# Opening gates of a row tile: sums by width chunk, first loads on two queues, a shorter warm-up

## The chip, the cores and the metric

The kernel runs on one core of one Trainium2 chip. The metric is the device time of one execution in microseconds (us); medians over several executions are given.

## The reference

```python
x = A_x                                   # 2048 rows x 640, bf16
xn = layernorm(x)                         # no scale, no bias
s = attention(xn, k_cache, v_cache, wq, wo)     # 32 heads of 192, last 512 keys
g = silu( (sigmoid(xn @ w_gate) * (xn @ w_up)) @ w_down )   # inner width 1536
return x + s * g
```

Only the gated part, and of it only the first block of 512 rows, is touched here. The width of 640 is five chunks of 128. The inner width of 1536 is twelve pieces of 128; the first four are called f = 0 to 3.

## The kernel before

TensorE is the bound. The kernel does the gated part first, because it needs only x and three weights, and hides the loads for attention behind it. At the very start nothing has been loaded yet, so the first 512 rows are opened row tile by row tile (128 rows each): `tile_gates` computes the first four pieces of the gate and up products of one row tile as soon as its rows are normalized and transposed. When all four tiles are in, the normal 512-row matmuls take over (`gated`).

The loads at the start, all on SyncE's queue:

```python
        nc.vector.memset(warm[:], 0.0)
        load_x(0, 1)
        load_x(1, 1)
        for f0, f1 in ((0, 4), (4, 8), (8, NF)):
            load_f(nc.sync, wg_sb, wg_r, f0, f1)
            load_f(nc.sync, wu_sb, wu_r, f0, f1)
            if f0 == 0:
                load_x(2, 1)
                load_x(3, 1)
```

The warm-up matmuls, the transpose of one row tile by TensorE with its copy out of PSUM (the memory that holds the sums of matmuls, `bank` in the code), and the opening of one row tile:

```python
        def dummy(n):
            for _ in range(n):
                nc.tensor.matmul(bank[2][:, 1, 0:256], lhsT=warm[:, 0:P], rhs=warm[:, 0:256],
                                 start=True, stop=True)
        # ... row statistics (stats_half, stats_end) and normalization (normal): VectorE ...
        def turn_pe(t, c0, c1, bk, eng):
            pT = bk[:, 0:NCD * H2].bitcast(BF16).rearrange("p (c n) -> p c n", c=NCD)
            for c in range(c0, c1):
                nc.tensor.transpose(pT[:, c, :], ln[t][:, c * P:(c + 1) * P], ident[:])
            dst = xnT[:, 0, c0:c1, t * P:(t + 1) * P]
            if eng is nc.vector:
                nc.vector.tensor_copy(dst, pT[:, c0:c1, :])
            else:
                nc.scalar.activation(dst, pT[:, c0:c1, :], AF.Copy)
        # ... cut ...
        def tile_gates(t, amid):

            if 0 not in hT:
                hT[0] = hpool.tile([P, NF, TB], BF16, name="hT")
            k = t % 3
            r = slice(t * P, (t + 1) * P)
            for half, w in ((0, wg_sb), (1, wu_sb)):
                for f in range(FT):
                    if (half, f) == (1, 2) and amid is not None:
                        turn_pe(amid, 0, NCD, bank[3][:, amid % 2, :], nc.scalar)
                    for c in range(NCD):
                        nc.tensor.matmul(bank[k][:, half, f * P:(f + 1) * P],
                                         lhsT=w[:, c, f * P:(f + 1) * P], rhs=xnT[:, 0, c, r],
                                         start=(c == 0), stop=(c == NCD - 1))
            sig = bwork.tile([P, TB], BF16, name="sig")
            nc.scalar.activation(sig[:], bank[k][:, 0, :], AF.Sigmoid)
            nc.vector.tensor_tensor(hT[0][:, 0:FT, r],
                                    bank[k][:, 1, :].rearrange("p (f n) -> p f n", f=FT),
                                    sig[:].rearrange("p (f n) -> p f n", f=FT), ALU.mult)
```

The program order of the opening, which is also the order on each engine:

```python
        dummy(20)
        full_stats(0)
        normal(0, ((0, 3 * P), (3 * P, D)))
        turn_pe(0, 0, 3, bank[3][:, 0, :], nc.vector)
        turn_pe(0, 3, NCD, bank[2][:, 0, :], nc.scalar)
        dummy(2)
        stats_half(1, 1)
        stats_end(1)
        normal(1)
        full_stats(2)
        tile_gates(0, 1)
        normal(2)
        full_stats(3)
        tile_gates(1, 2)
        normal(3)
        tile_gates(2, 3)
        tile_gates(3, None)
        k = 1
        for f in range(FT, NF):
            gated(0, f, k, norm_piece(1, f - FT))
            k = (k + 1) % 4
        # ... the rest of the kernel: unchanged ...
```

The softmax here doesn't subtract the row's maximum and nothing guards it: scores larger than these inputs give would overflow.

Of the kernel before, what the change touches and what calls it, by code (L numbers as in the profile page):

```python
# [8 lines left out]
AF = mybir.ActivationFunctionType  # L9
ALU = mybir.AluOpType  # L10
BF16 = mybir.dt.bfloat16
# [4 lines left out]
def kernel(  # L16
# [13 lines left out]
    nc = tc.nc  # L30
    P = 128
    H2 = 64
# [16 lines left out]
    NCD = D // P  # L49
    NF = F // P  # L50
# [19 lines left out]
    bank = [psum.tile([P, 2, 512], F32, name=f"bank{i}") for i in range(4)]  # L70
# [4 lines left out]
    ident = const.tile([P, P], BF16, name="ident")  # L75
# [3 lines left out]
    warm = const.tile([P, 512], BF16, name="warm")  # L79

    xnT = pers.tile([P, NB, NCD, TB], BF16, name="xnT")
# [5 lines left out]
    wg_r = B_w_gate.rearrange("(c p) f -> p c f", p=P)  # L87
    wu_r = B_w_up.rearrange("(c p) f -> p c f", p=P)
# [45 lines left out]
    with ExitStack() as bctx:  # L134
# [5 lines left out]
        wg_sb = wB.tile([P, NCD, F], BF16, name="wg_sb")  # L140
        wu_sb = wB.tile([P, NCD, F], BF16, name="wu_sb")
# [4 lines left out]
        def load_x(t, n):  # L146

            x = xpool.tile([P, n, D], BF16, name=f"x_sb{n}", bufs=4 if n == 1 else 2)
            nc.sync.dma_start(x[:], xf[t * P:(t + n) * P, :].rearrange("(q p) d -> p q d", p=P))  # L149
            for i in range(n):  # L150
                xt[t + i] = x[:, i, :]

        def load_f(eng, w, r, f0, f1):
            eng.dma_start(w[:, :, f0 * P:f1 * P], r[:, :, f0 * P:f1 * P])  # L154

        nc.vector.memset(warm[:], 0.0)
        load_x(0, 1)
        load_x(1, 1)
        for f0, f1 in ((0, 4), (4, 8), (8, NF)):
            load_f(nc.sync, wg_sb, wg_r, f0, f1)  # L160
            load_f(nc.sync, wu_sb, wu_r, f0, f1)
            if f0 == 0:
                load_x(2, 1)
                load_x(3, 1)
        load_x(TQ, TQ)
        nc.sync.dma_start(wd_sb[:], wd_r)
        load_x(2 * TQ, TQ)
# [6 lines left out]

        def dummy(n):
            for _ in range(n):
                nc.tensor.matmul(bank[2][:, 1, 0:256], lhsT=warm[:, 0:P], rhs=warm[:, 0:256],
                                 start=True, stop=True)

        ln = {}  # L180

        def stats_half(t, i):
            if i == 0:
                ln[t] = bwork.tile([P, 2, nc.vector.BN_STATS_DIM], F32, name="st")
            nc.vector.bn_stats(ln[t][:, i, :], xt[t][:, i * (D // 2):(i + 1) * (D // 2)])

        def stats_end(t):
            mv = bwork.tile([P, nc.vector.BN_AGGR_DIM], F32, name="mv")
            rstd = bwork.tile([P, 1], F32, name="rstd")
            nc.vector.bn_aggr(mv[:], ln[t][:])  # L190
            if t == 0:
                nc.scalar.activation(rstd[:], mv[:, 1:2], AF.Sqrt, bias=eps_t[:], scale=1.0)
                nc.scalar.activation(junk[:], eps_t[:], AF.Sigmoid)
                stats_half(1, 0)
                nc.vector.reciprocal(rstd[:], rstd[:])
            else:
                nc.vector.tensor_scalar(rstd[:], mv[:, 1:2], eps, None, op0=ALU.add)
                nc.gpsimd.tensor_tensor(rstd[:], rstd[:], mhalf[:], ALU.pow)
            ln[t] = mv, rstd

        def normal(t, parts=((0, D),)):
            mv, rstd = ln[t]
            xn = xpool.tile([P, D], BF16, name="xn")
            for d0, d1 in parts:
                nc.vector.tensor_scalar(xn[:, d0:d1], xt[t][:, d0:d1], mv[:, 0:1], rstd[:, 0:1],
                                        op0=ALU.subtract, op1=ALU.mult)
            ln[t] = xn

        def turn_pe(t, c0, c1, bk, eng):
            pT = bk[:, 0:NCD * H2].bitcast(BF16).rearrange("p (c n) -> p c n", c=NCD)  # L210
            for c in range(c0, c1):
                nc.tensor.transpose(pT[:, c, :], ln[t][:, c * P:(c + 1) * P], ident[:])  # L212
            dst = xnT[:, 0, c0:c1, t * P:(t + 1) * P]
            if eng is nc.vector:
                nc.vector.tensor_copy(dst, pT[:, c0:c1, :])
            else:
                nc.scalar.activation(dst, pT[:, c0:c1, :], AF.Copy)  # L217

        def turn_dma(t):
            q = t % TQ  # L220
# [2 lines left out]
        hT = {}  # L223
# [41 lines left out]
        FT = 4  # L265

        def tile_gates(t, amid):

            if 0 not in hT:
                hT[0] = hpool.tile([P, NF, TB], BF16, name="hT")  # L270
            k = t % 3
            r = slice(t * P, (t + 1) * P)
            for half, w in ((0, wg_sb), (1, wu_sb)):
                for f in range(FT):
                    if (half, f) == (1, 2) and amid is not None:
                        turn_pe(amid, 0, NCD, bank[3][:, amid % 2, :], nc.scalar)
                    for c in range(NCD):
                        nc.tensor.matmul(bank[k][:, half, f * P:(f + 1) * P],  # L278
                                         lhsT=w[:, c, f * P:(f + 1) * P], rhs=xnT[:, 0, c, r],
                                         start=(c == 0), stop=(c == NCD - 1))  # L280
            sig = bwork.tile([P, TB], BF16, name="sig")
            nc.scalar.activation(sig[:], bank[k][:, 0, :], AF.Sigmoid)
            nc.vector.tensor_tensor(hT[0][:, 0:FT, r],
                                    bank[k][:, 1, :].rearrange("p (f n) -> p f n", f=FT),
                                    sig[:].rearrange("p (f n) -> p f n", f=FT), ALU.mult)

        def full_stats(t):
            stats_half(t, 0)
            stats_half(t, 1)
            stats_end(t)  # L290

        dummy(20)
        full_stats(0)
        normal(0, ((0, 3 * P), (3 * P, D)))
        turn_pe(0, 0, 3, bank[3][:, 0, :], nc.vector)
        turn_pe(0, 3, NCD, bank[2][:, 0, :], nc.scalar)
        dummy(2)
        stats_half(1, 1)
        stats_end(1)
        normal(1)  # L300
        full_stats(2)
        tile_gates(0, 1)
        normal(2)
        full_stats(3)
        tile_gates(1, 2)
        normal(3)
        tile_gates(2, 3)
        tile_gates(3, None)
        k = 1
        for f in range(FT, NF):  # L310
            gated(0, f, k, norm_piece(1, f - FT))
            k = (k + 1) % 4
        for b in range(1, NB):
            for f in range(2):
                gated(b, f, k)
                k = (k + 1) % 4
            for q in range(TQ):
                down(b - 1, q, k)
                k = (k + 1) % 4
            if b == 1:  # L320
                load_x(3 * TQ, TQ)
            for f in range(2, NF):
                gated(b, f, k, norm_piece(b + 1, f - 4) if b + 1 < NB and f >= 4 else None)
                k = (k + 1) % 4
# [4 lines left out]
        for q in range(TQ):  # L329
            down(NB - 1, q, k)  # L330
            k = (k + 1) % 4
# [12 lines left out]
        for m in range(DJ):  # L344
# [3 lines left out]
            k = (k + 1) % 4  # L348
# [168 lines left out]
```

## Time and profile before

| | before |
|---|---|
| time, median of 4 runs of the first comparison | 931.91 us |
| span of the profiled run | 930.2 us |
| first gate matmul of tile 0 starts | 6.94 us |
| first 512-row gate matmul starts | 18.53 us |

By the profile's page TensorE is busy 922.3 of 930.2 us (99%). The view by windows of the kernel before shows where the rest is (columns: start and end in us, length, then busy time and instruction count of TensorE's matmuls, its weight loads, VectorE, ScalarE and GpSimd, then the granted TensorE clock, the DMA engines' share and GB/s).

```profile
0.00:19.00 19.00, 16.17 (x205) 13.91 (x206) 9.29 (x27) 7.49 (x13) 2.53 (x12) 1.00 0.95 303
19.00:920.00 901.00, 901.00 (x7796) 529.67 (x7795) 451.44 (x702) 296.98 (x318) 123.92 (x142) 1.00 0.36 77
```

Between 19 and 920 us TensorE is busy all the time. So whatever the change does, it can only move the moment at which this full stretch begins.

Next the timeline of TensorE's matmuls in the opening. The columns are: start, length, engine and line, operation, output<-inputs, shape, how many are merged into the row, and in brackets how long the engine was idle before it and what ended the idle time. Line 177 is the warm-up, 212 the transposes, 278 `tile_gates`, 231 the 512-row matmuls. The ends of matmuls are modelled, so the distance between starts is what to read. The warm-up matmuls multiply zeros and yield no result.

```profile
6.64 0.46 PE L177 MATMUL bank<-warm 128*128 128x256 bf16 x2 [0.47 <-ACT xnT L217]
6.94 1.28 PE L278 MATMUL bank<-xnT,wg_sb 128*128 128x128 bf16 x20
8.69 0.73 PE L278 MATMUL bank<-xnT,wu_sb 128*128 128x128 bf16 x10 [0.47 <-DMA wu_sb<-in_B_w_up_dram]
...
9.53 0.72 PE L278 MATMUL bank<-xnT,wu_sb 128*128 128x128 bf16 x10
10.49 1.28 PE L278 MATMUL bank<-xnT,wg_sb 128*128 128x128 bf16 x20 [0.23 <-ACT xnT L217]
...
13.39 1.28 PE L278 MATMUL bank<-xnT,wg_sb 128*128 128x128 bf16 x20 [0.23 <-ACT xnT L217]
...
18.53 0.38 PE L231 MATMUL bank<-xnT,wg_sb 128*128 128x512 bf16 x1
```

The first gate matmuls start at 6.94 us. The 20 of them need 1.1 us, so they are issued by 8.05; the up matmuls start at 8.69, after a wait for `wu_sb`. After every group of transposes only ten matmuls are left, and the next tile then waits for ScalarE's copy (`ACT xnT`). Gate matmuls of the four tiles start 3.55, 2.90 and 2.91 us apart. Without any wait a tile would need 45 matmuls of 0.0557 us, 2.51 us. Note also the two warm-up matmuls at 6.64: they wait 0.47 us for ScalarE, because they write into the PSUM buffer whose other half ScalarE is still reading.

The chain of waits (start, length, what; read it as the one path that ended last, in order of time) names the same things:

```profile
2.14 6.50 DMA wu_sb<-in_B_w_up_dram
...
8.69 0.73 PE bank L278 x10
...
9.73 0.71 ACT xnT L217
```

The path runs through the transfer of the up weights, issued at 2.14 and landed at 8.64 us, and then through ScalarE's copies of 0.71 us.

### The profile page before, as it was taken

The page shows a single profiled execution, that of the slowest core. Times are in us where ns is not written, and L with a number is a line of the kernel's source. Part 1 is how long each engine was busy: PE and PEld are TensorE (multiplying, and loading weights), DVE is VectorE, ACT ScalarE, POOL GpSimd, SP SyncE. Part 2 cuts the span into 40 slices and gives each one's busy share as a digit, 9 for nine tenths or more (in the row PEclk, how much of TensorE's full clock was granted, in tenths as well). Part 3 has the DMA queues.
Part 4 walks back from the last instruction along what each step waited for, and adds up shares of the span by engine and source line. Part 5 has one row for each costly group of instructions (what it writes and reads, how often), then busy time and mean ns, then how long its engine had stood idle before and what let it go on. Part 6 is the DMA issues. An engine that isn't in the chain of part 4 may idle for free.

```text
span 930.2 us, 18111 instructions
## 1 busy us (share of the span) xinstructions
PE 922.3 (99%) x8036; PEld 546.3 (59%) x8036; DVE 467.5 (50%) x738; ACT 304.5 (33%) x330; POOL 126.5 (14%) x154
## 2 busy tenths in 40 slices
PE   8999999999999999999999999999999999999997
PEld 6445455566655666655566655566666666666665
DVE  5452522454544544554554455445555555445657
ACT  3222222433333333333333333333333333333341
POOL 1000010400010002000200020002000205565000
PEclk9999999999999999999999999999999999999999
DMA  9310420616223433433343433263327234522223
GB/s 314 83 22 8 112 61 1 195 36 138 59 52 78 105 83 61 77 83 99 67 78 58 122 69 78 54 127 69 78 47 133 69 69 78 92 63 63 52 65 102
DMA packets 157807, 76.69 MB, mean 82 GB/s; under 512 B 140784, under 2 KB 151648, under 8 KB 157728
## 3 DMA queue, kind: packets, MB, share of 16 engines
q1 hardware_dynamic: 149904, 46.56, 25.4%
q0 software_dynamic: 7248, 28.38, 10.8%
q8 instruction: 63, 1.03, 0.5%
q10 hardware_dynamic: 576, 0.59, 0.2%
q14 instruction: 16, 0.13, 0.1%
HBM read 39.45 MB, written 2.62 MB: 45 GB/s over the span
## 4 chain that ended last, share of the span: by engine, by line
PE 97%; DVE 1%; DMA 1%; ACT 0%; SPq 0%; issue 0%; DVEq 0%
PE bank L390 22%; PE bank L427 21%; PE bank L407 19%; PE bank L372 18%; PE bank L231 10%; PE bank L243 6%; PE bank L278 1%; DMA wu_sb<-in_B_w_up_dram 1%; PE bank L340 1%; DVE gate L436 1%; DVE o_sb L431 1%; ACT xnT L217 0%; PE bank L212 0%; SPq L149 0%; SPq L154 0%
## 5 line engine op out<-in xcount | busy, mean ns | idle before, releaser
L376 ACT ACTIVATE E<-bank 128x1024 bf16<-128x1024 f32 x256 | 257.9, 1023 | 477.4 <-PE bank L372 453.5
L390 PE MATMUL bank<-xnT,wq_sb 64*128 64x512 bf16 x1860 | 231.4, 376 | 0.0
L427 PE MATMUL bank<-wo_sb,oT 128*128 128x512 bf16 (+1 forms) x1536 | 228.6, 299 | 0.0
L372 PE MATMUL bank<-qT,kT 64*128 64x512 bf16 x1536 | 202.2, 377 | 0.0
L407 PE MATMUL bank<-vbuf,E 128*128 128x193 bf16 x2048 | 191.0, 247 | 0.0
L407 PEld LDWEIGHTS <-E 128*128 128x128 bf16 x2048 | 167.8, 98 | 24.2 <-issue 13.6
L397 DVE CAST qT<-bank 128x1024 bf16<-128x1024 f32 x93 | 113.9, 1224 | 132.8 <-PE bank L390 132.8
L427 PEld LDWEIGHTS <-oT 128*128 128x128 bf16 x1536 | 121.1, 98 | 76.9 <-issue 0.4
L390 PEld LDWEIGHTS <-wq_sb 64*128 64x128 bf16 x1860 | 97.2, 100 | 104.6
L372 PEld LDWEIGHTS <-kT 64*128 64x128 bf16 x1536 | 72.9, 94 | 90.1 <-issue 8.8
L413 DVE TENSOR_TENSOR o_st<-bank,rden 128x768 bf16<-128x768 f32 x128 | 122.5, 957 | 4.4
L442 DVE TENSOR_TENSOR acc<-bank,acc 128x640 f32<-128x640 f32 x96 | 79.1, 824 | 43.8 <-PE bank L427 43.8
L395 DVE COPY seen<-bank 128x2 f32<-128x2 f32 x93 | 14.8, 159 | 93.9 <-PE bank L390 93.8
L412 DVE RECIPROCAL rden<-bank 128x4 f32<-128x4 f32 x128 | 23.3, 182 | 71.4 <-PE bank L407 71.4
L231 PE MATMUL bank<-xnT,wg_sb 128*128 128x512 bf16 x220 | 54.7, 379 | 0.0
L231 PE MATMUL bank<-xnT,wu_sb 128*128 128x512 bf16 x220 | 54.7, 379 | 0.0
L243 PE MATMUL bank<-wd_sb,hT 128*128 128x512 bf16 (+1 forms) x384 | 52.8, 299 | 0.0
L237 DVE TENSOR_TENSOR hT<-bank,sig 128x512 bf16<-128x512 f32 x44 | 30.3, 689 | 43.7 <-ACT sig L234 43.7
L234 ACT ACTIVATE sig<-bank 128x512 bf16<-128x512 f32 x44 | 26.3, 597 | 68.4 <-PE bank L231 63.8
L106 POOL DMA_DIRECT2D vbuf<-in_A_v_cache_dram x28 | 20.9, 748 | 184.9 <-PE bank L407 184.9
L243 PEld LDWEIGHTS <-hT 128*128 128x128 bf16 x384 | 29.6, 98 | 23.2
L231 PEld LDWEIGHTS <-wu_sb 128*128 128x128 bf16 x220 | 21.5, 98 | 26.0
(50 smaller groups left out, 277.6 us busy)
## 6 DMA issues: line engine op xcount, KB each, us to landing
wo_sb<-in_A_wo_dram POOLq DMA_DIRECT2D x8, 960.0 KB, 7.4
wq_sb<-in_A_wq_dram POOLq DMA_DIRECT2D x7, 960.0 KB, 6.3
k_st<-in_A_k_cache_dram POOLq DMA_DIRECT2D x7, 768.0 KB, 8.0
vbuf<-in_A_v_cache_dram POOLq DMA_DIRECT2D x28, 192.0 KB, 3.0
row<-in_A_x_dram POOLq DMA_DIRECT2D x16, 160.0 KB, 2.6
oT<-o_st SPq DMA_TRANSPOSE x128, 2.6
wg_sb<-in_B_w_gate_dram SPq DMA_DIRECT2D x3, 640.0 KB, 7.4
wu_sb<-in_B_w_up_dram SPq DMA_DIRECT2D x3, 640.0 KB, 8.5
```

The costliest lines, as they stand in the source:

```text
L231: nc.tensor.matmul(bank[k][:, half, 0:r1 - r0], lhsT=w[:, c, f * P:(f + 1) * P], rhs=xnT[:, b, c, r0:r1], start=(c == 0), stop=(c == NCD - 1))
L234: nc.scalar.activation(sig[:, 0:r1 - r0], bank[k][:, 0, 0:r1 - r0], AF.Sigmoid)
L237: nc.vector.tensor_tensor(hT[b][:, f, r0:r1], bank[k][:, 1, 0:r1 - r0], sig[:, 0:r1 - r0], ALU.mult)
L243: nc.tensor.matmul(wide(k)[:, d0:d1], lhsT=hT[b][:, f, q * P:(q + 1) * P], rhs=wd_sb[:, f, d0:d1], start=(f == 0), stop=(f == NF - 1))
L372: nc.tensor.matmul(bank[k][:, i, :], lhsT=kT[r, pr, j, c * P:(c + 1) * P], rhs=q[r, pr * DJ + j, :], start=(j == 0), stop=(j == DJ - 1))
L376: nc.scalar.activation(E[u, pr][:, c, :, :], bank[k][:], AF.Exp, scale=scale_qk)
L390: nc.tensor.matmul(bank[k][:, half, :], lhsT=wq[r, c, col:col + DJ * (P - 1) + 1:DJ], rhs=xnT[r, b, c, :], start=(c == 0 and not second), ...
L397: nc.vector.tensor_copy(qT[u][:, 2 * m:2 * m + 2, :], bank[k][:])
L407: nc.tensor.matmul(o4[:, q, 0:DH + 1], lhsT=e[:, c, h % 2, q * P:(q + 1) * P], rhs=v[:, h, c, 0:DH + 1], start=(c == 0), stop=(c == KC - 1))
L413: nc.vector.tensor_tensor(o_st[u][:, :, h * DH:(h + 1) * DH], o4[:, :, 0:DH], rden[:].to_broadcast([P, TQ, DH]), ALU.mult)
L427: nc.tensor.matmul(wide(k)[:, d0:d1], lhsT=oT[u][:, cc, q * P:(q + 1) * P], rhs=wo[:, cc, d0:d1], start=(cc == 0), stop=(cc == GC - 1))
L442: nc.vector.tensor_tensor(acc[:, t, :], wide(k)[:, 0:D], acc[:, t, :], ALU.add)
```

## The change

The intent: let TensorE start on the first row tile earlier and without holes. Matmuls go chunk by chunk of the width, so that the first three chunks can start on a part of the copies and of the up weights. All four pieces share one PSUM bank, and only the first matmul into the bank carries the clearing flag. The Trainium skill, "PSUM — Partial Sum Buffer", section "The four PSUM rules", says that this flag clears the written-marks of the whole bank, so that later first writes overwrite and the rest add up; a flag per piece would undo the other pieces' sums. The first gate weights move to ScalarE's queue; a small memset into their tile makes that transfer wait for VectorE. The up weights come in two transfers, with x tile 2 between. Transposes of the next tile move to another place, their copy is in two parts, and the first half of the statistics of tile 2 comes ahead of the normalized rows of tile 1.

```diff
--- before.py
+++ after.py
@@ -150,18 +150,22 @@
             for i in range(n):
                 xt[t + i] = x[:, i, :]
 
-        def load_f(eng, w, r, f0, f1):
-            eng.dma_start(w[:, :, f0 * P:f1 * P], r[:, :, f0 * P:f1 * P])
+        def load_f(eng, w, r, f0, f1, c0=0, c1=NCD):
+            eng.dma_start(w[:, c0:c1, f0 * P:f1 * P], r[:, c0:c1, f0 * P:f1 * P])
 
         nc.vector.memset(warm[:], 0.0)
+
+        nc.vector.memset(wg_sb[:, 0, 0:2], 0.0)
         load_x(0, 1)
         load_x(1, 1)
-        for f0, f1 in ((0, 4), (4, 8), (8, NF)):
+        load_f(nc.scalar, wg_sb, wg_r, 0, 4)
+        load_f(nc.sync, wu_sb, wu_r, 0, 4, 0, 3)
+        load_x(2, 1)
+        load_f(nc.sync, wu_sb, wu_r, 0, 4, 3, NCD)
+        load_x(3, 1)
+        for f0, f1 in ((4, 8), (8, NF)):
             load_f(nc.sync, wg_sb, wg_r, f0, f1)
             load_f(nc.sync, wu_sb, wu_r, f0, f1)
-            if f0 == 0:
-                load_x(2, 1)
-                load_x(3, 1)
         load_x(TQ, TQ)
         nc.sync.dma_start(wd_sb[:], wd_r)
         load_x(2 * TQ, TQ)
@@ -174,7 +178,7 @@
 
         def dummy(n):
             for _ in range(n):
-                nc.tensor.matmul(bank[2][:, 1, 0:256], lhsT=warm[:, 0:P], rhs=warm[:, 0:256],
+                nc.tensor.matmul(bank[1][:, 1, 0:256], lhsT=warm[:, 0:P], rhs=warm[:, 0:256],
                                  start=True, stop=True)
 
         ln = {}
@@ -206,15 +210,21 @@
                                         op0=ALU.subtract, op1=ALU.mult)
             ln[t] = xn
 
-        def turn_pe(t, c0, c1, bk, eng):
-            pT = bk[:, 0:NCD * H2].bitcast(BF16).rearrange("p (c n) -> p c n", c=NCD)
-            for c in range(c0, c1):
-                nc.tensor.transpose(pT[:, c, :], ln[t][:, c * P:(c + 1) * P], ident[:])
-            dst = xnT[:, 0, c0:c1, t * P:(t + 1) * P]
-            if eng is nc.vector:
-                nc.vector.tensor_copy(dst, pT[:, c0:c1, :])
-            else:
-                nc.scalar.activation(dst, pT[:, c0:c1, :], AF.Copy)
+        def turn_pe(t):
+
+            engs = (nc.vector, nc.scalar) if t == 0 else (nc.scalar, nc.scalar)
+            parts = []
+            for i, (c0, c1) in enumerate(((0, 3), (3, NCD))):
+                bk = bank[3][:, t % 2, :] if t or i == 0 else bank[2][:, 0, :]
+                pT = bk[:, 0:NCD * H2].bitcast(BF16).rearrange("p (c n) -> p c n", c=NCD)
+                for c in range(c0, c1):
+                    nc.tensor.transpose(pT[:, c, :], ln[t][:, c * P:(c + 1) * P], ident[:])
+                parts.append((engs[i], xnT[:, 0, c0:c1, t * P:(t + 1) * P], pT[:, c0:c1, :]))
+            for eng, dst, src in parts:
+                if eng is nc.vector:
+                    nc.vector.tensor_copy(dst, src)
+                else:
+                    nc.scalar.activation(dst, src, AF.Copy)
 
         def turn_dma(t):
             q = t % TQ
@@ -270,42 +280,50 @@
                 hT[0] = hpool.tile([P, NF, TB], BF16, name="hT")
             k = t % 3
             r = slice(t * P, (t + 1) * P)
+
+
+
             for half, w in ((0, wg_sb), (1, wu_sb)):
-                for f in range(FT):
-                    if (half, f) == (1, 2) and amid is not None:
-                        turn_pe(amid, 0, NCD, bank[3][:, amid % 2, :], nc.scalar)
-                    for c in range(NCD):
+                for c in range(NCD):
+                    if half == 1 and c == amid:
+                        turn_pe(t + 1)
+                    for f in range(FT):
                         nc.tensor.matmul(bank[k][:, half, f * P:(f + 1) * P],
                                          lhsT=w[:, c, f * P:(f + 1) * P], rhs=xnT[:, 0, c, r],
-                                         start=(c == 0), stop=(c == NCD - 1))
+                                         start=(c == 0 and f == 0), stop=(c == NCD - 1),
+                                         skip_group_check=True)
             sig = bwork.tile([P, TB], BF16, name="sig")
             nc.scalar.activation(sig[:], bank[k][:, 0, :], AF.Sigmoid)
-            nc.vector.tensor_tensor(hT[0][:, 0:FT, r],
-                                    bank[k][:, 1, :].rearrange("p (f n) -> p f n", f=FT),
-                                    sig[:].rearrange("p (f n) -> p f n", f=FT), ALU.mult)
-
-        def full_stats(t):
-            stats_half(t, 0)
-            stats_half(t, 1)
-            stats_end(t)
-
-        dummy(20)
-        full_stats(0)
+            return lambda: nc.vector.tensor_tensor(
+                hT[0][:, 0:FT, r], bank[k][:, 1, :].rearrange("p (f n) -> p f n", f=FT),
+                sig[:].rearrange("p (f n) -> p f n", f=FT), ALU.mult)
+
+        dummy(18)
+        stats_half(0, 0)
+        stats_half(0, 1)
+        stats_end(0)
         normal(0, ((0, 3 * P), (3 * P, D)))
-        turn_pe(0, 0, 3, bank[3][:, 0, :], nc.vector)
-        turn_pe(0, 3, NCD, bank[2][:, 0, :], nc.scalar)
+        turn_pe(0)
         dummy(2)
         stats_half(1, 1)
         stats_end(1)
+        stats_half(2, 0)
         normal(1)
-        full_stats(2)
-        tile_gates(0, 1)
+        stats_half(2, 1)
+        stats_end(2)
+        stats_half(3, 0)
+        stats_half(3, 1)
         normal(2)
-        full_stats(3)
-        tile_gates(1, 2)
+        stats_end(3)
+        m0 = tile_gates(0, 3)
+        m0()
         normal(3)
-        tile_gates(2, 3)
-        tile_gates(3, None)
+        m1 = tile_gates(1, 1)
+        m1()
+        m2 = tile_gates(2, 1)
+        m2()
+        m3 = tile_gates(3, None)
+        m3()
         k = 1
         for f in range(FT, NF):
             gated(0, f, k, norm_piece(1, f - FT))
```

## The prediction

> **What bounds the kernel now.** Of a span of 930.2 us the tensor engine is busy 922.3 (99%, the table of engines). The stage table by windows shows it busy 779.0 of 779.0 us between 141 and 920 us and 122.0 of 122.0 between 19 and 141. The changed kernel has the same instructions there in the same order. So only the start of the first 512-row gate matmul can move (18.48 us in the timeline of before), and all later work with it.
>
> **The opening of before** (timeline, chain of waits): 20 warm-up matmuls from 1.19 us, 0.21 us apart; transposes of tile 0 from 5.2 us; first gate weight load at 6.82 us, just when the gate weights have landed; 20 gate matmuls, about 56 ns apart; then 0.64 us of waiting for the up weights (the chain names this transfer from 2.14 to 8.64 us). Tiles 0 to 3 then each end with a stall of about 0.35 us on ScalarE's copy of the next transposed tile (0.70 us; only ten matmuls, 0.55 us, cover it), three times. The stalls make 1.7 of the 11.66 us from 6.82 to 18.48.
>
> **What the change does.**
> 1. Chunk-outer order: same matmul count, no cost. The first 12 up matmuls need only the first up transfer (384 KB).
> 2. Transposes of the next tile: 16 matmuls (0.88 us) now cover the copy for tiles 2 and 3, 8 (0.44 us) for tile 1, and the copy is in two parts (0.4 us each). Those stalls fall from 3 x 0.35 to about 0.2 in total: gain 0.85 us.
> 3. Up weights in two parts, the second behind x tile 2: the wait of 0.64 us in the middle of tile 0 should vanish: gain 0.6 us.
> 4. Gate weights on ScalarE's queue, issued after a 0.06 us memset, at about 1.25 instead of 1.67 us. But the Trainium skill, "DMA: Bandwidth & Descriptors", section "Issuing engines are not separate DMA queues", says such transfers run on the same 16 engines and interleave. The DMA strip of before agrees: about 350 GB/s without a gap from 4 us on. The gate weights now share them with up weights and x tile 2 (0.55 MB) that were behind them. From these rates I estimate the landing, and the first gate load, at 7.3 us (6.4 to 8) instead of 6.82: loss 0.5 us.
> 5. Two warm-up matmuls fewer (0.43 us), and the last two no longer wait for ScalarE: transposes 0.1 to 0.3 us earlier, hidden behind the weights.
>
> Sum: 0.85 + 0.6 - 0.5, plus 0.3 if the earlier issue brings all transfers forward: gain 1.3 us.
>
> **Predicted: 930.7 us, 929.7 to 931.9. Faster by over 2%: 0.5%; within 2%: 99%; slower by over 2%: 0.5%.**
>
> **What would show it.** The first 512-row gate matmul at about 17.2 us, all later groups unchanged in mean and count; first gate weight load at about 7.3 us waiting for a DMA; no wait for the up weights; at most one short wait for a tile copy.
>
> **What would make it wrong.** Gate weights landing near 6.4 us (gain over 2 us) or after 8.5 us (no gain). The clock: matmuls are 0.21 us apart before about 6.8 us and at full pace after. The skill's "TensorE: Matmul & The Clock Gate", Part 1, puts the release at a window of about 3.4 us of sustained work; if the thinner warm-up misses that window, up to about 3.4 us of gate matmuls run at half pace, a loss of 1.7 us.

## The result

The prediction's time and range held: 930.15 us against 930.7 (929.7 to 931.9). But the range reaches up to the time of the kernel before (931.91), so it would have held with almost no gain too; the steps are the real test. Ratios in this document are the mean time of one kernel's runs over that of the other's of the same rounds, so not quite the ratio of the medians.

| | before | changed |
|---|---|---|
| median, first comparison (4 runs each) | 931.91 us | 930.15 us |
| ratio, 95% interval | | 0.9987, 0.997 to 1.0005 |
| median, second comparison (9 and 5 runs) | 932.13 us | 929.94 us |
| ratio, 95% interval | | 0.998, 0.9967 to 0.9994 |
| first gate matmuls of tiles 0, 1, 2, 3 start | 6.94, 10.49, 13.39, 16.30 us | 6.67, 9.61, 12.12, 14.63 us |
| first 512-row gate matmul starts | 18.53 us | 16.86 us |

One of the first four runs of the changed kernel took 932.55 us, with a mean granted clock of 0.997 where the others have 1.0; it alone pulls the ratio of the first comparison up. The interval of the first comparison includes 1, that of the second does not.

The changed kernel's view by windows, columns as above:

```profile
0.00:19.00 19.00, 17.37 (x210) 14.02 (x211) 9.84 (x29) 8.22 (x16) 2.53 (x12) 1.00 0.96 309
19.00:920.00 901.00, 901.00 (x7800) 530.20 (x7799) 452.63 (x703) 296.65 (x317) 123.91 (x142) 1.00 0.35 77
```

The middle stretch is as full as before. In the first 19 us TensorE is busy 1.2 us more. Its timeline (line 181 is the warm-up, 221 the transposes, 291 `tile_gates`, 241 the 512-row matmuls):

```profile
6.67 1.29 PE L291 MATMUL bank<-xnT,wg_sb 128*128 128x128 bf16 x20 [0.31 <-DMA wg_sb<-in_B_w_gate_dram]
7.79 0.83 PE L291 MATMUL bank<-xnT,wu_sb 128*128 128x128 bf16 x12
8.57 0.45 PE L221 MATMUL bank<-ident,xn 128*128 128x128 bf16 x5
8.86 0.61 PE L291 MATMUL bank<-xnT,wu_sb 128*128 128x128 bf16 x8
9.61 1.28 PE L291 MATMUL bank<-xnT,wg_sb 128*128 128x128 bf16 x20
...
12.12 1.28 PE L291 MATMUL bank<-xnT,wg_sb 128*128 128x128 bf16 x20
...
16.86 0.38 PE L241 MATMUL bank<-xnT,wg_sb 128*128 128x512 bf16 x1
```

The up matmuls follow the gate matmuls without a wait (6.67 plus 20 times 0.056 is 7.79). Tiles 1 and 2 take 2.51 us each, which is the bare count of matmuls. Tile 0 takes 2.94, so 0.43 us of waits are left there. The chain of waits of the changed kernel goes from the landing of the gate weights through the transposes and one copy, and meets no up weights any more:

```profile
1.19 5.43 DMA wg_sb<-in_B_w_gate_dram
...
6.67 1.96 PE bank L291 x32
8.63 0.41 PE bank L221 x5
...
9.06 0.50 ACT xnT L227
```

Comparing the two timelines start by start: the first gate matmul comes 0.27 us earlier, tile 0 is 0.61 us shorter, tile 1 0.39 and tile 2 0.40. The sum is 1.67 us; the spans differ by 1.8 (930.2 and 928.4). The rest, about 0.1 us, I have not placed.

### The profile page after: what moved, and what is told of

Its sections match the earlier page's. It is cut to its first block, busy times and chain, and to the rows that moved or that the text cites. A ratio compares the mean times of both kernels' runs of the same rounds, so it can differ in the third digit from the quotient of the medians.

```text
span 928.4 us, 18112 instructions
## 1 busy us (share of the span) xinstructions
PE 921.9 (99%) x8034; PEld 546.1 (59%) x8034; DVE 467.7 (50%) x739; ACT 304.9 (33%) x333; POOL 126.4 (14%) x154
## 4 chain that ended last, share of the span: by engine, by line
PE 98%; DVE 1%; DMA 1%; issue 0%; ACT 0%; DVEq 0%
PE bank L408 22%; PE bank L445 21%; PE bank L425 19%; PE bank L390 18%; PE bank L241 10%; PE bank L253 6%; PE bank L291 1%; PE bank L358 1%; DVE gate L454 1%; DMA wg_sb<-in_B_w_gate_dram 1%; DVE o_sb L449 1%; PE bank L221 0%; ACT xnT L227 0%; DVEq L530 0%; DVE warm L156 0%
```

## The experiments

Each kernel was run five times with the kernel before beside it on the same chip (nine runs of it). Medians of the kernel before were 932.12, 932.13, 932.05 and 931.93 us in the four batches, so a few tenths between batches mean nothing. The intervals of the ratios reach about 0.13%, or 1.2 us, to either side, so a difference under a microsecond is read together with the waits in the traces. All results were correct.

Theory A, formed from the two traces: the parts of the change lean on each other. The new order pays only because x tile 2 and the up weights come earlier, and the early loads pay only because the order needs them in that sequence. What holds the opening is a landing: of the gate weights, of the up weights or of x tile 2. Rival B: the parts are worth their own gains, which add up, as my prediction summed them.

### The new order alone

The changed kernel with the loads of before, `dummy(20)` and the warm-up in its old PSUM buffer:

```diff
-        load_f(nc.scalar, wg_sb, wg_r, 0, 4)
-        load_f(nc.sync, wu_sb, wu_r, 0, 4, 0, 3)
-        ...                      (all loads of the change, and the memset)
+        for f0, f1 in ((0, 4), (4, 8), (8, NF)):     (as in the kernel before)
-        dummy(18)
+        dummy(20)
```

> The changed kernel with the loads and the warm-up of before (only the order of matmuls, transposes, copies and row work is new). Theory A (the parts lean on each other: x tile 2 now gates the normalized rows of tile 1, because the half statistics of tile 2 stand ahead of them on VectorE; with before's loads x tile 2 lands near 9.06 us): the wait for the up weights stays (about 0.6 us), the transposes of tile 1 come near 10 us and stall TensorE again; gain against before 0.3 to 0.7 us, first 512-row gate matmul at 17.8 to 18.2 us. Rival B (the parts add up; my prediction's sum): the copy stalls fall by 0.85 us, gain 0.8 us or more, first 512-row matmul at 17.7 us or earlier.

Measured: 932.19 us against 932.12, ratio 0.9999 (0.9985 to 1.0012). By the median the new order alone is worth nothing, less than either expectation. The profiled run, one of the quicker ones (931.78 us), starts the 512-row matmuls at 18.37 us, within 0.2 of before. Its chain of waits:

```profile
2.71 6.46 DMA x_sb<-in_A_x_dram
...
9.19 0.49 DVE st L185
9.68 0.36 DVE xn L205
...
10.09 0.47 PE bank L217 x5
```

x tile 2 lands at 9.16 us here. Its statistics (`DVE st`) stand ahead of the normalized rows of tile 1 (`DVE xn`) in VectorE's program, so tile 1, whose own rows were there long before, waits for x tile 2. VectorE works in order, and what was put in front of tile 1 became its wait. Tile 0 grows to 4.25 us, and the gain of the shorter tiles 1 and 2 is lost there. The wait for the up weights is there as well (0.60 us). The path is theory A's, and it costs more than I wrote.

### The new loads alone

The kernel before with only the load statements of the change (and its memset):

```diff
-        for f0, f1 in ((0, 4), (4, 8), (8, NF)):     (the loads of before)
+        nc.vector.memset(wg_sb[:, 0, 0:2], 0.0)
+        load_f(nc.scalar, wg_sb, wg_r, 0, 4)
+        load_f(nc.sync, wu_sb, wu_r, 0, 4, 0, 3)
+        ...                      (as in the change)
```

> The kernel before with the loads of the change only (gate weights on ScalarE's queue, up weights in two transfers, x tile 2 between). Theory A: gate weights land near 6.6 us, the second up transfer near 8.4 us; the old order needs all of the up weights 1.1 us after the first gate matmul, so a wait of 0.3 to 0.5 us remains; the three copy stalls of 0.35 us remain; gain 0.3 to 0.6 us. Rival B (parts add up): 0.6 us or a little more, no wait for the up weights.

Measured: 931.47 us against 932.12, ratio 0.999; all five runs lie between 931.31 and 931.53. The medians differ by 0.65 us, at the edge of both expectations. The timeline tells them apart (line 181 warm-up, 216 transposes, 282 `tile_gates`):

```profile
6.65 0.38 PE L181 MATMUL bank<-warm 128*128 128x256 bf16 x2 [0.47 <-ACT xnT L221]
6.87 1.28 PE L282 MATMUL bank<-xnT,wg_sb 128*128 128x128 bf16 x20
7.98 0.33 PE L282 MATMUL bank<-xnT,wu_sb 128*128 128x128 bf16 x3
8.47 0.56 PE L282 MATMUL bank<-xnT,wu_sb 128*128 128x128 bf16 x7 [0.16 <-DMA wu_sb<-in_B_w_up_dram]
```

There is still a wait inside the up matmuls: three are issued from 7.98 us, the rest from 8.47, when the second up transfer has landed. The old order needs all five chunks for its first piece. The copy waits are all there, tile 0 takes 3.24 us. And the gate weights had landed by 6.1 us (issued at 1.19, 4.9 us to landing), but the first gate matmul waits until 6.87: the two old warm-up matmuls sit in front of it, waiting for ScalarE. So in this trace the old order and the warm-up's old buffer keep the kernel from using the loads (the buffer was never changed alone). Order alone gives about nothing, loads alone 0.65 us, the whole change 1.8 to 2.2 us, and the wait that rival B said would be gone is there. Rival B falls.

### Gate weights back on SyncE's queue

```diff
-        load_f(nc.scalar, wg_sb, wg_r, 0, 4)
+        load_f(nc.sync, wg_sb, wg_r, 0, 4)
```

> The changed kernel with the first gate weights back on SyncE's queue, third in it as before. Theory A (each queue's transfer is mostly drained in order of issue, so what ScalarE's queue bought is the 0.48 us earlier issue): landing at 6.7 to 6.8 us, x tile 2 and up weights later too; 0.15 to 0.4 us slower than the changed kernel, about 930.3 to 930.6 us. Rival (sharing, step 4 of the prediction: two queues split the 16 engines and that holds the gate weights back): alone in front they land at 6.4 us or earlier and the time is 0.1 us or more below the changed kernel.

Measured: 931.23 us, runs from 930.22 to 932.2, against 932.12 before. The kernel with 20 warm-up matmuls, which differs from the changed one in nothing that counts (next experiment), had 930.07 in the same rounds, so by the medians the queue is worth about 1 us: the direction is theory A's, the size is above its 0.15 to 0.4. The size is loose, because the two sets of five runs overlap (930.22 and 930.63) and the edit also issues all transfers behind the gate weights 0.4 to 0.5 us later. The rival, which was step 4 of my prediction, falls: alone on one queue the gate weights landed not earlier but at 7.38 us (theory A had 6.7 to 6.8). One landing proves little, since it varies from trace to trace, but none of the five runs is below 930.07 either. The packets show what was wrong in step 4. In the changed kernel, from 4 to 5 us, by queue (q10 is ScalarE's, q1 SyncE's; packets, MB, share of the 16 engines' time):

```profile
q10 hardware_dynamic: 349, 0.36, 101.0%
q1 hardware_dynamic: 17, 0.02, 4.9%
```

Transfers had been issued on both queues from 1.67 us on, but almost all of this microsecond went to the transfer that had been issued first. This is no rule that the engines share unevenly. In the kernel with 20 warm-up matmuls at the end of the experiments, which splits the gate weights too, the first up transfer and the second gate transfer are issued together, at about 1.7 us, and from 5 to 6 us the queues move

```profile
q1 hardware_dynamic: 192, 0.19, 54.7%
q10 hardware_dynamic: 169, 0.17, 49.5%
```

So two transfers that are under way together did split the engines about evenly. What step 4 had wrong is that they would be under way together: in the changed kernel the up weights, issued 0.48 us after the gate weights, moved in earnest only from 5 us on (262 packets of SyncE's queue from 5 to 6 us), when the gate weights were nearly through. Why they start so late the traces do not show.

The profiled run is also the longest of the five (932.2 us, mean clock 0.998), and it caught one kind of long run. Timeline and windows of it:

```profile
7.42 1.80 PE L291 MATMUL bank<-xnT,wg_sb 128*128 128x128 bf16 x20 [1.45 <-DMA wg_sb<-in_B_w_gate_dram]
9.02 1.49 PE L291 MATMUL bank<-xnT,wu_sb 128*128 128x128 bf16 x12
10.30 0.74 PE L221 MATMUL bank<-ident,xn 128*128 128x128 bf16 x5
```

```profile
4.60:8.00 3.40, 1.72 (x21) 1.08 (x20) 1.90 (x7) 1.72 (x3) 0.57 (x1) 1.00 1.08 356
8.00:11.40 3.40, 3.40 (x36) 3.40 (x34) 2.33 (x8) 0.33 (x1) 0.56 (x1) 0.50 1.09 353
```

The clock stands at 0.50 of full speed from 8.0 to 11.4 us, and at 1.00 in the windows on both sides. From the first gate matmul to the first up matmul it takes 1.60 us, and the twelve up matmuls take 1.28 us (0.107 us each), where the full clock needs 1.12 and 0.67. In the 3.4 us before, TensorE was busy only 1.72 us, because it waited for the gate weights. The Trainium skill, "TensorE: Matmul & The Clock Gate", Part 1, describes a clock gate that judges TensorE's activity in free-running windows of about 3.4 us; the stretch of 3.4 us agrees with that length.

### Twenty warm-up matmuls again

```diff
-        dummy(18)
+        dummy(20)
```

> The changed kernel with 20 warm-up matmuls again instead of 18. Theory A: the first gate matmul waits for its weights at 6.6 us either way, the transposes move by 0.2 us and stay hidden: 930.1 us, within 0.1 of the changed kernel, and no run with a late release of the clock. Rival: the shorter warm-up is worth 0.2 us or more of itself, so this is 930.3 us or more.

Measured: 930.07 us, runs 929.97 to 930.63, ratio 0.9976 (0.9964 to 0.9989); no run with a clock of 0.998 or less. The shorter warm-up of itself is worth nothing that can be seen. In this trace the clock was already free at the transposes, and the gate weights had landed by 5.9 us:

```profile
6.12 1.28 PE L291 MATMUL bank<-xnT,wg_sb 128*128 128x128 bf16 x20
...
8.36 0.45 PE L221 MATMUL bank<-ident,xn 128*128 128x128 bf16 x5 [0.30 <-DVE xn L209]
```

The first gate matmul starts 0.55 us earlier than in the changed kernel's first trace, yet tile 1 starts only 0.22 us earlier. Between them stands a wait of 0.30 us for the normalized rows of tile 1, and the chain of waits of this run goes through x tile 2, as it does in the next run. When the gate weights land in good time, x tile 2 holds the opening.

### The changed kernel once more

No edit; the changed kernel is run again with other kernels beside it.

> The changed kernel once more, to see how its time and its opening vary. Theory A (two things vary between executions, whatever the warm-up: when the first gate weights land, 6.1 to 7.4 us in the traces so far, and in which window the clock is released): most runs 929.9 to 930.6 us, none to two of five late in clock (0.998 or less) and 1.5 us or more longer. Rival (the shorter warm-up makes late clocks frequent): three or more of five late in clock.

Measured: 929.94 us against 932.13, four runs between 929.89 and 930.13 and one of 933.31 with a clock of 0.997. The chain of waits:

```profile
2.14 5.44 DMA x_sb<-in_A_x_dram
...
7.61 0.49 DVE st L189
```

Together with the first comparison two of nine runs of the changed kernel have a clock of 0.997, and both are over 2 us longer than the others; of the kernel before, three of 36 in the four batches have 0.997, and these three are the longest (933.48 to 933.75). Two more of these have 0.998 at a usual time (932.13 and 932.02), so 0.998 alone does not mark a long run. Nor does the mean clock show a slow start: in the run with ten warm-up matmuls, below, the view by windows gives 1.00 from 5.2 to 7.9 us, where the matmuls run at half pace. These numbers are too small to call one more frequent than the other, but they speak against the rival's three or more of five. That the runs at 0.997 are of the kind traced above is likely from their clock, but none of them was traced.

### Up weights in one transfer

```diff
-        load_f(nc.sync, wu_sb, wu_r, 0, 4, 0, 3)
-        load_x(2, 1)
-        load_f(nc.sync, wu_sb, wu_r, 0, 4, 3, NCD)
+        load_f(nc.sync, wu_sb, wu_r, 0, 4)
+        load_x(2, 1)
```

> The changed kernel with the first up weights in one transfer, x tile 2 behind it. Theory A: what the two transfers buy is above all the earlier x tile 2; here it lands 0.5 us later, the normalized rows of tile 1 (behind its half statistics on VectorE) come after 9 us, and the transposes of tile 1 hold TensorE up: 0.4 to 0.8 us slower than the changed kernel, about 930.7 us, with the wait in front of the transposes. Rival (my prediction: it removes the wait for the up weights): a wait of up to 0.6 us for the up weights in front of the first up matmul, and none in front of the transposes.

Measured: 931.05 us against 929.94 for the changed kernel in the same batch, so 1.1 us slower, more than the 0.4 to 0.8 expected. Both waits are there. In the trace the up matmuls start at 7.85 instead of 7.39 us (the rival's wait, 0.46), but the path goes through x tile 2, which lands at 8.3 instead of 7.6 us:

```profile
2.14 6.16 DMA x_sb<-in_A_x_dram
...
8.32 0.49 DVE st L188
...
9.22 0.47 PE bank L220 x5
```

Tile 1 starts 0.71 us later than in the changed kernel's trace of the same batch (10.25 and 9.54); the spans of the two differ by 0.7 us as well, so of the 1.1 us between the medians this trace places 0.7. The wait for the up weights is not on this path: with or without it, the transposes of tile 1 would have waited for x tile 2 until 9.22 us. What this trace shows of the worth of the two transfers is theory A's.

### Without the memset

```diff
-        nc.vector.memset(wg_sb[:, 0, 0:2], 0.0)
```

> The changed kernel without the small memset that holds the first gate weights back: they are issued near 0.75 us, beside x tile 0. Theory A: x tile 0 lands up to 0.5 us later, the row work of tile 0 starts later, the gate weights land near 6 us; the first gate matmul then waits for the transposed rows instead: within 0.3 us of the changed kernel. Rival (the memset only delays): first gate matmul and end 0.3 us or more earlier.

Measured: 932.52 us, 2.6 us slower than the changed kernel and no better than before. My theory named the right mechanism and missed the size, and the tile: x tile 0 was hardly later, x tile 1 was.

```profile
1.20 4.68 DMA x_sb<-in_A_x_dram
...
5.90 0.49 DVE st L188
...
6.93 0.54 PE bank L220 x5
```

Without the memset the gate weights are issued at 0.74 us, beside x tile 0. x tile 1, issued at 1.20, lands only at 5.88 us, after the whole of the gate weights (0.74 plus 4.7 us). With the memset it took 2.8 to 3.0 us instead of 4.68. The first half of its statistics stands in VectorE's program ahead of the last step of tile 0's statistics, so tile 0 waits too, and the transposes begin at 6.93 instead of 5.21 us. This is the quickest of the five runs, and its span is 1.1 us longer than that of the changed kernel's trace (929.5 and 928.4); the rest of the 2.6 us lies in the four slower runs, which were not traced. Of the single edits undone here, this memset of 0.06 us, which holds a large transfer back by 0.45 us, until two small ones are issued, costs most.

### Rows of tile 1 ahead of the statistics of tile 2

```diff
-        stats_half(2, 0)
         normal(1)
+        stats_half(2, 0)
...
-        m0 = tile_gates(0, 3)
+        m0 = tile_gates(0, 2)
```

> The changed kernel with the normalized rows of tile 1 ahead of the first statistics of tile 2 on VectorE, and the transposes of tile 1 after two up chunks instead of three. Theory A: tile 1's start loses its waits (0.13 us for the rows, 0.30 us for ScalarE's copy in the trace of the changed kernel): 0.3 to 0.4 us faster, about 929.8 us; gate matmuls of tile 1 start 2.6 us after those of tile 0 instead of 2.94. Rival: the wait is ScalarE's or the up weights' and stays: no change.

Measured: 929.9 us against 929.94 in the same batch, ratio to before 0.9976. The three short runs are 929.80 to 929.90, so at most 0.1 us is gained, not 0.3 to 0.4. The profiled run is the longest one (931.22 us): the gate weights landed at 8.00 us there, 6.8 us after their issue. The lateness is that of the last packets: after 6 us only 19 of 656 were left, among 678 of SyncE's queue up to 8 us.

```profile
8.05 1.29 PE L291 MATMUL bank<-xnT,wg_sb 128*128 128x128 bf16 x20 [1.56 <-DMA wg_sb<-in_B_w_gate_dram]
...
10.64 1.28 PE L291 MATMUL bank<-xnT,wg_sb 128*128 128x128 bf16 x20
```

In this run tile 1 starts 2.59 us after tile 0, as expected: the wait behind x tile 2 is gone, and only 0.08 us is left. But a late landing hides what a normal run does, so why the median did not move by 0.3 us this trace can't say. This is the second kind of long run: the clock stays at 1.00 (0.999 for the run), although TensorE waits for the gate weights even longer than in the run on SyncE's queue (1.56 us and 1.45). So the length of the wait does not decide by itself whether the clock falls.

### Ten warm-up matmuls

```diff
-        dummy(18)
+        dummy(10)
```

> The changed kernel with 10 warm-up matmuls instead of 18: TensorE idles from about 3.3 to 5.2 us. Window theory (the clock is released and kept by how busy TensorE is in windows of 3.41 us, the length of the half-clock stretch in the trace with the late clock): most runs lose one window, so three or more of five are 1.5 us or more longer than the changed kernel, with gate matmuls 0.107 us apart in the trace; median 931.5 us or more. Rival (late clocks come at random, in about one of eight runs so far, whatever the warm-up): median within 0.2 us of the changed kernel, 930.0 us.

Measured: 931.49 us, runs 931.05 to 931.79 (before: 932.05). Against the changed kernel's 929.94 (another batch) the median is 1.5 us longer, and four of the five runs are 1.5 us or more longer; the two kernels with 20 warm-up matmuls of the same batch (next section) have 930.07 and 930.05. The timeline of the profiled run:

```profile
1.19 2.32 PE L181 MATMUL bank<-warm 128*128 128x256 bf16 x10 [1.19 <-DVE eps_t L172]
...
6.22 2.09 PE L291 MATMUL bank<-xnT,wg_sb 128*128 128x128 bf16 x20
8.15 0.83 PE L291 MATMUL bank<-xnT,wu_sb 128*128 128x128 bf16 x12
```

The gate matmuls start at 6.22 us as usual but need 1.93 us to the first up matmul, 0.1 us each: they run at half pace. From then on the spacing is 0.056 us. In the other traces the full pace began no later than about 7 us. So the warm-up does work, ten matmuls are too few, and 18 did as well as 20. The rival falls. The half pace is what the window theory expected; that the clock acts in windows, this run alone does not show. The profiled run is a mild case: the 512-row matmuls start at 17.10 us, so it lost 0.3 us in the span (928.7 us; about a microsecond of its time of 931.47 lies outside the span). The other four runs have spans of 929.3 to 929.8 us, against 928.1 to 928.4 of the changed kernel's usual runs; they were not traced.

### Both edits, then the gate weights in two transfers

The next kernel has 20 warm-up matmuls and the edit for the rows of tile 1:

```diff
-        dummy(18)
+        dummy(20)
-        stats_half(2, 0)
         normal(1)
+        stats_half(2, 0)
-        m0 = tile_gates(0, 3)
+        m0 = tile_gates(0, 2)
```

> Both edits that helped or did no harm: 20 warm-up matmuls, normalized rows of tile 1 first, transposes of tile 1 after two up chunks. If they add up: 929.6 to 929.9 us, first 512-row gate matmul at 16.3 us, no late clock. If the second up transfer or x tile 3 lands too late for the earlier start: as the changed kernel, 929.9 to 930.1 us, with a wait for a transfer in tile 0 or tile 1.

Measured: 930.07 us, runs 929.66 to 933.12, ratio 0.9985 (before 932.05). Nothing is gained over the changed kernel, and two runs are long (931.13, and 933.12 at a clock of 0.998). In the trace the wait for x tile 2 is gone from the chain, but the warm-up took its place: 20 matmuls at half clock, then transposes, copy, statistics and rows of tile 1, whose transposes begin at 8.38 us against 8.36 in the run with 20 warm-up matmuls above. A second path of about the same length lay right behind the first.

The last two split the gate weights as well, with 20 and with 18 warm-up matmuls:

```diff
-        load_f(nc.scalar, wg_sb, wg_r, 0, 4)
+        load_f(nc.scalar, wg_sb, wg_r, 0, 4, 0, 3)
+        load_f(nc.scalar, wg_sb, wg_r, 0, 4, 3, NCD)
```

> As the kernel with 20 warm-up matmuls and the rows of tile 1 first, but the first gate weights too in two transfers (three chunks, then two). If the landing of the gate weights holds the start: first gate matmul at 6.1 us, when the transposed rows are there, in every run, time 929.4 to 929.7 us and fewer long runs. If the up weights then hold it instead (they share the engines): a wait of 0.2 to 0.5 us in front of the first up matmul and no gain.

Measured with 20: 930.05 us, all five runs between 929.97 and 930.12, ratio 0.9977 (0.9965 to 0.999). It is not faster than the changed kernel, and the first gate matmul starts at 6.52 us, not at 6.1, but no run is long. Its chain of waits is TensorE alone: the 20 warm-up matmuls of 4.45 us to 5.64, transposes to 6.29, two more warm-up matmuls, then the gate matmuls.

> The last kernel, a candidate for the best: first gate weights in two transfers, rows of tile 1 first, transposes of tile 1 after two up chunks, and 18 warm-up matmuls as in the change. With 20 the chain of waits ran through the warm-up alone (20 matmuls, 4.45 us, then transposes, then two more), so two fewer should move everything by 0.2 to 0.4 us: 929.6 to 929.9 us, first gate matmul near 6.2 us, and again no run over 930.5 us, since no run waits for the whole of the gate weights. If the warm-up was not what held it: 930.0 us as before.

Measured with 18, on another chip: 930.66 us against 931.93, runs 929.98 to 930.88. The expectation failed. In the trace the first gate matmul does start at 6.23 us, but the second gate transfer lands at 8.04 us and TensorE waits 1.1 us for it in the middle of the gate matmuls:

```profile
1.68 6.37 DMA wg_sb<-in_B_w_gate_dram
...
8.09 1.07 PE bank L292 x16
```

In both traces this transfer is the one that shares the engines with the up weights. With 20 it landed at about 7.3 us. Whether the chip or two warm-up matmuls made that difference was not tested. None of these kernels beats the changed one clearly, so it stands.

## Why the prediction was right

- **Only the opening counts: right.** TensorE is busy 901.0 of 901.0 us in the middle in both traces, and the span shrank by what the opening lost, 1.67 of 1.8 us.
- **Step 2, the copy waits: right in size (0.85 predicted, 0.75 measured: 1.40 for tiles 0 to 2, less the 0.65 of step 3), not in the cause of what is left.** Tiles 1 and 2 lost their waits (0.39 and 0.40 us). Tile 0's stayed, and it is not only ScalarE's copy: before the transposes stands a wait for the rows of tile 1, which stand on VectorE behind x tile 2. I did not see this path. The order alone (ratio 0.9999) and the up weights in one transfer (1.1 us slower) showed it.
- **Step 3, the wait for the up weights: right.** 0.65 us in the trace of before (from 8.04 to 8.69), none after. With the up weights in one transfer part of the wait is back, but there x tile 2 is the longer path.
- **Step 4, the gate weights on ScalarE's queue: the mis-sized term.** I put the first gate load at 7.3 us, a loss of 0.5 us, because I let the gate weights share the engines with the up weights and x tile 2. It came at 6.66 us, a gain; the first gate matmul moved by 0.27 us, and in the later traces it is at 6.1 to 6.3 us where the landing was in time. The skill's statement that the transfers interleave on the same engines is not contradicted: two transfers issued together moved 192 and 169 packets in a microsecond. But here the gate weights were hardly shared: 349 packets to 17. Back on SyncE's queue the weights landed at 7.38 us in the trace, and the kernel lost about 1 us.
- **Step 5, the warm-up: right for the count (18 or 20 is the same), incomplete for the buffer.** I called the earlier transposes hidden. With the new loads the old warm-up's wait for ScalarE would have held the first gate matmul until 6.87 us, although its weights had landed by 6.1.
- **The sum.** 0.85 + 0.6 - 0.5 + 0.3 was 1.3 us; measured 0.75 + 0.65 + 0.27 is 1.67. That the sum came so near is partly luck: step 4 has the wrong sign, and the 0.3 us that I added for earlier issue hid part of its error. The second comparison, with the weights landing at 6.0 us in its trace, gained 2.2 us, which the prediction had named as a way to be wrong (6.4 us, over 2 us).
- **The clock: a true risk, with another cause than I named.** By their clock of 0.997 it probably struck two of nine runs of the changed kernel and three of 36 of the kernel before. In the one traced case, with the gate weights on SyncE's queue, TensorE had been idle for half a window because weights landed late; whether two more warm-up matmuls would have kept the clock up was not tested.

## What to carry to other kernels

When the start of a kernel is held by landings, the order of issue on the queues and the order of work on the in-order engines are one design: a step that waits for a later transfer must not stand in front of a step that does not, and small early loads must be protected from large ones. Test the parts of such a change alone before you add up their gains, since here order alone gave nothing and loads alone a third. And look for the second path of equal length before you shorten the first.

## What the Trainium skill lacked or had wrong

- "TensorE: Matmul & The Clock Gate", Part 1, gives one idle window of about 3.4 us as the condition for falling back to half clock. Here the clock fell to 0.50 after a stretch of 3.40 us in which TensorE was busy 1.72 us with 21 matmuls, so half a window of work did not keep it. No page that I read says how much work does: in another run a wait of 1.56 us, longer than the 1.45 us here, left the clock at 1.00.
- "DMA: Bandwidth & Descriptors", section "Issuing engines are not separate DMA queues", says that transfers of several engines interleave and that a second issuing engine saves only issue time. The first fits where two transfers were issued together (192 packets to 169 in 1 us), but the section lacks when a transfer comes under way: one issued 0.48 us after another moved 17 packets to its 349. Moving one 640 KB transfer to ScalarE's queue saved about 0.5 us of issue and was worth about 1 us by the medians of five runs each, which overlap; that is too loose to call the second wrong.
- No page that I read gives the spread of landings: the same 640 KB transfer, issued at 1.19 us behind the same loads, took 4.6 to 6.8 us to land in the traces.
- No page that I read says what a large transfer issued at the same time does to a small one: x tile 1 (160 KB) took 4.68 us to land behind gate weights issued 0.46 us before it, and 2.8 to 3.0 us where both were issued at about 1.2 us; the kernel lost 2.6 us.
